# SwiGLU's first token group: block products of 256 columns in place of plain products of 512

## The chip, the cores and the metric

One Trainium2 chip (trn2), one of its cores. The metric is the device time of one execution in microseconds (us); lower is better.

## The reference

Three stages run one after the other on 2304 tokens (4 batches of 576) of width 512, in float32:

```python
q_s = softmax(q, axis=-1);  k_s = softmax(k, axis=2)          # with 1e-9 in the sums
x = einsum('bhsd,bhde->bhse', q_s, einsum('bhsd,bhse->bhde', k_s, v))   # 8 heads of 64
...
P = exp(x @ w_gate - max)                                     # 8 rounds of row and column scaling
for e in range(8):
    out += P[:, e:e+1] * (np.maximum(x @ w1[e], 0) @ w2[e])   # 512 -> 1024 -> 512
...
xn = x / np.sqrt(np.mean(x * x, -1) + 1e-6) * rms_g
g = xn @ w_gate;  val = xn @ w_val                            # 512 -> 1536
return (g / (1 + exp(-g)) * val) @ w_out                      # 1536 -> 512 (SwiGLU)
```

## The kernel before, in words

**Numbers in two halves.** Every large product is made of three matmuls: an operand is split into a high half (a copy rounded to fp32r) and a low half (what is left), and `mm3` (line 97) adds high x high, high x low and low x high in PSUM. So lines 98, 99 and 100 are nearly all of TensorE's work.

**Groups and units.** The 2304 tokens are cut into three groups of 512, 896 and 896 (`GP` holds half of each: 256, 448, 448). The hidden dimension is cut into chunks of 256: 32 units for each group in the mixture of experts (units 0 to 95), 6 for each group in SwiGLU (units 96 to 101 for the first group, 102 to 107, 108 to 113). A unit has two parts: `h`, its first products with what makes the hidden activations, and `y`, the second product that is added to the output rows. Parts stand in the program as h(u+1), y(u), h(u+2), y(u+1): the y of a unit lies behind the h of the next. Units 64 to 107 are one such stretch.

**Plain products and seven for eight.** The first token group takes its first products plainly: `plain` (line 824) multiplies chunk halves of 128 hidden columns with 512 tokens at a time, 24 matmuls for each weight matrix of a unit. The other groups use `seven` (line 772): the weights and the tokens are cut into 2 x 2 blocks, sums of blocks are formed beforehand, and seven block products (each 6 matmuls, here of 448 columns) stand for eight. What is left is put together from PSUM banks: `keep` copies a product on ScalarE, three additions run on VectorE (lines 795, 799, 804), one on GpSimd (line 805). Four banks are used: b1 twice, b2 and b3 once each. A product that adds to a bank waits until the copy from it is done, and one that takes a bank anew waits until the addition from it is done.

**SwiGLU units.** `unit2_h` (line 1019) does the gate matrix ("a"), then the value matrix ("v"). `gate_part` takes a sigmoid on ScalarE (line 1025) and multiplies on VectorE (line 1026); `value_part` multiplies (line 1029), rounds (line 1031) and takes the low half (line 1032). `unit2_y` adds into the output tiles (line 1077): 4 tiles of 128 tokens in the first group, 7 in the others.

**What is loaded when.** Block sums of tokens lie in seven tiles, `SX` (B11, T1, B21, T2, B22, T4, T3, in the order in which `seven` takes them). There is one buffer of each, so the sums of the next group can be loaded only when the last product of the group before has read its tile. In SwiGLU's second and third group they are read from DRAM by `sx_load` (line 718), 896 KB each. The block weights are read by `ws_load` (line 281), 896 KB for each half of a matrix, into two buffers; each load stands behind the product that frees its buffer. All these loads stand on one queue, SP, in the order of the program: an issue that has to wait holds up those behind it. The tokens of SwiGLU's first group come as plain halves from DRAM (`first_again`, line 975, into a slot kept as `X0`), written by `norm_first` (line 957) after the RMS norm of that group. Small steps (norms, block sums, second weights) are attached to places of units by `task` and `spread` (lines 1096 and 1222), called as `hook(i)`.

Of the kernel before, what the change touches and what calls it, by code (L numbers as in the profile page):

```python
# [18 lines left out]
def kernel(  # L19
# [260 lines left out]
    def ws_load(key):  # L280

        ws_alloc(key)
        for w, t in zip("hl", WS[key]):
            t = t.rearrange("p a k f -> p (a k f)").bitcast(F32)
            if key[1] < NU:
                nc.sync.dma_start(t, WSD[key + (w,)])
            else:
                g, c = divmod(key[1] - NU, NC2)
                d = WSD[key[0], c, w]
                if g:  # L290
                    nc.sync.dma_start(t, d[:, 2 * P:])
                else:
                    nc.sync.dma_start(t[:, :8 * P], d[:, :8 * P])
# [421 lines left out]
    def sx_alloc(nm, g):  # L715
        SX[nm] = sxp.tile([P, 2, 2, G], F32R, tag=nm, name=f"s{nm}_{g}")

    def sx_load(g, i):
        nm = NAMES[i]
        sx_alloc(nm, g)  # L720
        nc.sync.dma_start(SX[nm].rearrange("p w j n -> p (w j n)").bitcast(F32), SXD[nm, g])

    def sx_steps(g, j, b11, b21, b12, b22, stored):

        shp = b11.shape[1:]

# [3 lines left out]
        def put(nm, s):  # L730
            if stored:
                if j == 0:
                    SXD[nm, g] = dram.tile(
                        [P, 4 * G], F32, tag=f"{nm}{g}", name=f"sd{nm}_{g}"
# [3 lines left out]
                    f"{nm}_{g}_{j}", s, lambda t: v(t[:, :G]), lambda w: v(d[:, w, j]),  # L738
                    None if g == NG + 2 else staged,
# [32 lines left out]
    def seven(key, c, hook, after):  # L772

        wh, wl = WS.pop(key)
        nm = f"{key[0]}_{key[1]}"
        bk = {}
        tmp = {}

        def keep(n, i):
            tmp[n] = cp_.tile([P, G], F32, tag="u1" if n == "u3" else n, name=f"{n}_{nm}")  # L780
# [43 lines left out]
    def plain(u, f, key, stored):  # L824

        ph = bank("h", 2 * GP[0], f"ph_{key[0]}_{u}_{f}")
        plain_mm(ph, f, key, stored, range(KD))
        return ph

    def plain_mm(ph, f, key, stored, kks):  # L830
        wh, wl = WS[key]
        xh, xl = X0
        for kk in kks:
            if stored:
                i = ((2, 3), (0, 1))[f][kk // 2]
                lh, ll = wh[:, i, kk % 2], wl[:, i, kk % 2]
            else:
                lh, ll = (plain_view(t)[:, kk, f * P:(f + 1) * P] for t in (wh, wl))
# [10 lines left out]
    def unit_h(u, hook):  # L849
        if u < NCH:  # L850
            hook(0)
            for f in range(2):
                if f:
                    hook(1)
                if u == 0:
                    ph = FIRST_PH[f]
                    plain_mm(ph, f, ("a", 0), False, (KD - 1,))
                else:
                    ph = plain(u, f, ("a", u), False)
# [95 lines left out]
    XN0D = {}  # L955

    def norm_first(kk):

        pn = bank("y", DM, f"pn_0_{kk}")
        for t in range(TPG[0]):  # L960
            nc.tensor.transpose(
                pn[:, t * P:(t + 1) * P], ACC[0, 0][:, t, kk * P:(kk + 1) * P], ident
            )
        hi, lo = piece(f"xn0_{kk}")
        nc.scalar.activation(hi, pn, AF.Copy, scale=rmsg[:, kk:kk + 1])
        nc.vector.scalar_tensor_tensor(
            lo, pn, rmsg[:, kk:kk + 1], hi.bitcast(F32), op0=ALU.mult, op1=ALU.subtract
        )
        if kk == 0:
            XN0D[0] = dram.tile([P, 2 * KD * DM], F32, tag="xn0", name="xn0")  # L970
        d = XN0D[0].rearrange("p (w k n) -> p w k n", w=2, k=KD)
        for w, t in enumerate((hi, lo)):
            nc.sync.dma_start(d[:, w, kk], t.bitcast(F32))

    def first_again():
        nonlocal X0
        t = slot_a()
        nc.sync.dma_start(t.bitcast(F32), XN0D[0])
        X0 = as_x0(t)

# [4 lines left out]
    def norm_transpose(g, kk):  # L985
# [3 lines left out]
        for i in range(2):  # L989
# [14 lines left out]
        out_(0, 0, n, pns[0][:, :n * per])  # L1004
        out_(1, 0, 8 - n, pns[0][:, n * per:])
        out_(1, 8 - n, n, pns[1][:, :(2 * n - 8) * per])

    def norm_steps(g):
# [3 lines left out]
        if g == 0:  # L1012
            return steps + [lambda kk=kk: norm_first(kk) for kk in range(KD)]

# [4 lines left out]
    def unit2_h(u, hook):  # L1019
# [16 lines left out]
        cg = cp_.tile([P, 2, 2, G], F32, tag="c", name=f"cg_{u}")  # L1036
# [427 lines left out]
```

## Time and profile before

| | |
|---|---|
| device time, median of 3 runs | 2036.11 us (2035.25 to 2037.14) |
| the profiled execution, from its first to its last instruction (span) | 2033.2 us |
| median of the runs less that span | 2.9 us |
| TensorE matmuls | 2007.5 us busy, 99% of the span, 9522 instructions |
| VectorE, ScalarE, GpSimd | 69%, 38%, 20% of the span |
| DMA | 415 MB, mean 204 GB/s |

The profile gives the profiled execution by its span; it has no other time of its own. What lies around the span (2.9 us to the median) is taken as the same for both kernels. A matmul's record is longer than the distance to the next one, since matmuls overlap in the array; the distances of their starts tell what a stream of them costs.

### The profile page before, as it was taken

The numbers are of one execution on the slowest core, as the hardware profiler recorded it, in microseconds if no ns is written. First come the engines' busy times: TensorE is split into PE (matmuls) and PEld (weight loads), VectorE is DVE, ScalarE is ACT, GpSimd is POOL, SyncE is SP. The second block draws the span as 40 slices with busy tenths as digits, with TensorE's granted clock in tenths as the row PEclk, the third lists the DMA queues.
The fourth block names the chain that finished last, engine by engine and source line by source line (L and its number), as shares of the span: only waits on it lengthen the run. The fifth ranks groups of instructions, "written<-read, shape, count | busy, mean of one in ns | idle before, by whom it ended". The sixth has DMA issues, their size and how long they took to land.

```text
span 2033.2 us, 25609 instructions
## 1 busy us (share of the span) xinstructions
PE 2007.5 (99%) x9522; PEld 1739.5 (86%) x9522; DVE 1410.8 (69%) x2174; ACT 780.2 (38%) x1378; POOL 412.7 (20%) x388
## 2 busy tenths in 40 slices
PE   7999999999999999999999999999999999999999
PEld 5888888888888888888888888888888888888887
DVE  8775787776777777776658878878765446565455
ACT  5554333345333443343343333333332243432432
POOL 5541000022222222222113223223220000110110
PEclk9999999999999999999999999999999999999999
DMA  7443232355665665565677778878874747656542
GB/s 207 128 128 104 83 104 93 96 184 187 228 221 210 220 212 197 203 219 192 258 280 260 260 257 289 282 271 294 278 251 170 269 152 257 224 202 264 196 160 76
DMA packets 154236, 415.09 MB, mean 204 GB/s; under 512 B 13568, under 2 KB 66304, under 8 KB 153728
## 3 DMA queue, kind: packets, MB, share of 16 engines
q1 hardware_dynamic: 154112, 413.47, 58.7%
q8 instruction: 74, 1.21, 0.2%
q14 instruction: 50, 0.41, 0.1%
HBM read 281.69 MB, written 131.73 MB: 203 GB/s over the span
## 4 chain that ended last, share of the span: by engine, by line
PE 95%; DVE 4%; ACT 1%; issue 0%; DMA 0%; POOL 0%; DVEq 0%; POOLq 0%; ACTq 0%
PE py L98 13%; PE py L99 13%; PE py L100 13%; PE b_a L100 10%; PE b_a L99 10%; PE b_a L98 10%; PE ph_a L98 3%; PE ph_a L100 3%; PE ph_a L99 3%; PE po L98 2%; PE po L100 2%; PE po L99 2%; PE b_v L98 2%; PE b_v L100 2%; PE b_v L99 2%; PE pv L566 1%
## 5 line engine op out<-in xcount | busy, mean ns | idle before, releaser
L98 PE MATMUL py<-w2h,hh 128*128 128x512 f32 x1152 | 453.3, 393 | 3.4 <-DVE slot_e L905 1.9
L99 PE MATMUL py<-w2l,hh 128*128 128x512 f32 x1152 | 449.5, 390 | 0.0
L100 PE MATMUL py<-w2h,hl 128*128 128x512 f32 x1152 | 449.0, 390 | 0.0
L781 ACT COPY u_a<-b_a 128x448 f32<-128x448 f32 x228 | 121.6, 533 | 693.4 <-PE b_a L100 693.2
L98 PEld LDWEIGHTS py<-w2h,hh 128*128 128x128 f32 x1152 | 216.5, 188 | 47.5 <-DVE slot_e L905 2.1
L100 PEld LDWEIGHTS py<-w2h,hl 128*128 128x128 f32 x1152 | 216.6, 188 | 45.8
L99 PEld LDWEIGHTS py<-w2l,hh 128*128 128x128 f32 x1152 | 216.6, 188 | 42.9
L98 PE MATMUL b_a<-sT,wsh_a 128*128 128x448 f32 x608 | 220.0, 362 | 3.2 <-DVE c L795 2.1
L100 PE MATMUL b_a<-sT,wsl_a 128*128 128x448 f32 x608 | 220.7, 363 | 0.0
L99 PE MATMUL b_a<-sT,wsh_a 128*128 128x448 f32 x608 | 220.3, 362 | 0.0
L909 DVE SCALAR_TENSOR_TENSOR slot_a<-py,Pm,slot_a 128x512 f32<-128x512 f32 x217 | 162.4, 749 | 52.3 <-PE py L100 50.1
L909 DVE SCALAR_TENSOR_TENSOR slot_b<-py,Pm,slot_b 128x512 f32<-128x512 f32 x217 | 161.1, 745 | 23.6 <-PE py L100 22.5
L100 PE MATMUL b_a<-sB,wsl_a 128*128 128x448 f32 x456 | 165.7, 363 | 0.3 <-DMA wsl_a<-wdl_a 0.3
L99 PE MATMUL b_a<-sB,wsh_a 128*128 128x448 f32 x456 | 165.2, 362 | 0.0
L98 PE MATMUL b_a<-sB,wsh_a 128*128 128x448 f32 x456 | 165.2, 362 | 0.0
L95 DVE TENSOR_TENSOR w2l<-w2r,w2h 128x512 fp32r<-128x512 f32 x162 | 118.0, 729 | 41.4 <-ACT w2h L94 41.4
L805 POOL TENSOR_TENSOR c<-u_a,p_a 128x448 f32<-128x448 f32 x64 | 73.9, 1155 | 344.2 <-ACT u_a L781 344.1
L843 DVE SCALAR_TENSOR_TENSOR hl<-c,hh 128x896 fp32r<-128x896 f32 x128 | 143.0, 1117 | 0.9 <-ACT hh L842 0.7
L240 POOL TENSOR_TENSOR sum<-w1r 128x256 f32<-128x256 f32 x32 | 23.7, 741 | 565.2 <-DMA w1r<-in_moe_w_dram 247.1
L842 ACT ACTIVATE hh<-c 128x896 fp32r<-128x896 f32 x128 | 122.4, 956 | 27.9 <-POOL c L805 27.9
L94 ACT CAST w2h<-w2r 128x512 fp32r<-128x512 f32 x162 | 97.1, 618 | 88.9 <-PE py L100 80.7
L98 PEld LDWEIGHTS b_a<-sT,wsh_a 128*128 128x128 f32 x608 | 113.7, 187 | 13.1 <-DVE c L795 3.7
(232 smaller groups left out, 3675.4 us busy)
## 6 DMA issues: line engine op xcount, KB each, us to landing
w2r<-in_moe_w_dram SPq DMA_DIRECT2D x96, 512.0 KB, 4.6
w1r<-in_moe_w_dram SPq DMA_DIRECT2D x64, 512.0 KB, 3.5
wsdh<-wsh_a SPq DMA_DIRECT2D x32, 896.0 KB, 6.5
wsdl<-wsl_a SPq DMA_DIRECT2D x32, 896.0 KB, 7.9
wsh_a<-wsdh SPq DMA_DIRECT2D x32, 896.0 KB, 6.7
wsl_a<-wsdl SPq DMA_DIRECT2D x32, 896.0 KB, 8.4
w2d<-w2l SPq DMA_DIRECT2D x32, 512.0 KB, 2.9
w2l<-w2d SPq DMA_DIRECT2D x32, 512.0 KB, 4.8
```

The costliest lines, as they stand in the source:

```text
L94: nc.scalar.copy(hi, src)
L95: (eng or nc.vector).tensor_tensor(lo, src, hi.bitcast(F32), op=ALU.subtract)
L98: nc.tensor.matmul(ps, lh, rh, start=first, stop=False, skip_group_check=True)
L99: nc.tensor.matmul(ps, lh, rl, start=False, stop=False, skip_group_check=True)
L100: nc.tensor.matmul(ps, ll, rh, start=False, stop=last, skip_group_check=True)
L240: nc.gpsimd.tensor_tensor(s1, a21, a22, op=ALU.add)
L566: nc.tensor.matmul(st["pv"][:, :P], st["ke"][:, c].rearrange("p h d -> p (h d)"), st["v"][:, :, c, :], start=(c == 0), stop=(c == SC - 1),)
L781: nc.scalar.copy(tmp[n], bk[i])
L805: nc.gpsimd.tensor_tensor(c[:, 1, 1], tmp["u3"], tmp["p5"], op=ALU.add)
L842: nc.scalar.activation(th, src, AF.Relu)
L843: return lambda: nc.vector.scalar_tensor_tensor(tl, src, 0.0, th.bitcast(F32), op0=ALU.max, op1=ALU.subtract)
L909: nc.vector.scalar_tensor_tensor(a, py, pe, a, op0=ALU.mult, op1=ALU.add)
```

## The change

The first token group's SwiGLU units take `seven` as well, with block columns of 256 tokens: 42 matmuls of 256 columns for each matrix instead of 24 of 512. Its normed tokens are formed into block sums and stored in DRAM, seven pairs of halves, instead of the plain halves; `norm_first` and `first_again` go away. The weights' load is the same for all groups now (14 blocks instead of 8 for the first). The block sums of the first group are loaded in unit 95, tile by tile as its products free them (512 KB each), and those of the second group in the value products of unit 101 (hooks 7 to 13); before, those of the second group were all loaded at the start of unit 96. The sums of the first group take 51 small steps, which now lie in units 32 to 38 (before 16 steps in units 34 to 37), and the next group's first steps begin two units later.

```diff
@@ ws_load
-                g, c = divmod(key[1] - NU, NC2)
+                c = (key[1] - NU) % NC2
                 d = WSD[key[0], c, w]
-                if g:
-                    nc.sync.dma_start(t, d[:, 2 * P:])
-                else:
-                    nc.sync.dma_start(t[:, :8 * P], d[:, :8 * P])
+                nc.sync.dma_start(t, d[:, 2 * P:])
...
@@ sx_alloc, seven
+        w = GP[g % NG]
+        t = sxp.tile([P, 4 * G], F32R, tag=nm, name=f"s{nm}_{g}")[:, :4 * w]
...
-                bk[b] = pb_tile(f"b{b}", f"b{b}_{nm}_{i}")[:, :G]
+                bk[b] = pb_tile(f"b{b}", f"b{b}_{nm}_{i}")[:, :w_]
...
@@ norm_transpose, norm_steps
-        for i in range(2):
+        for i in range(1 if g == 0 else 2):
...
+        if g == 0:
+            out_(1, 0, n, pns[0][:, n * per:])
+            return
...
-        if g == 0:
-            return steps + [lambda kk=kk: norm_first(kk) for kk in range(KD)]
-
         steps += [lambda kk=kk: norm_transpose(g, kk) for kk in range(KD)]
         return steps + sx_all(g + NG, lambda kk, h: norm_place(g, kk, h), True)
...
@@ unit2_h
-        if g == 0:
-            for f in range(2):
-                hook(f)
-                to = cg[:, f].rearrange("p t g -> p (t g)")[:, :n]
-                gate_part(plain(u, f, ("a", u), True), to, f)
...
-            return
...
+        cg = four(cp_.tile([P, 2, 2, G], F32, tag="c", name=f"cg_{u}"))
+        cv = four(cp2.tile([P, 2, 2, G], F32, tag="cv", name=f"cv_{u}"))
         hook(-1)
         seven(("a", u), cg, hook, lambda f: gate_part(flat(cg, f), flat(cg, f), f))
...
@@ tasks
-            task("h", u, (0 if group(u)[0] == 0 else 4) + f, lambda u=u, f=f: w2_split(u, f))
+            task("h", u, 4 + f, lambda u=u, f=f: w2_split(u, f))
...
-    spread([("h", u, i) for u in range(34, 38) for i in (0, 1, 3, 4)], lambda: norm_steps(0))
+    spread(
+        [at for u in range(33, 39) for at in
+         [("h", u, i) for i in (0, 1, 3, 4)] + [("y", u - 1, i) for i in range(6)]][6:],
+        lambda: norm_steps(0),
+    )
...
-        [("y", u, i) for u in range(39, 57) for i in (3, 5)],
+        [("y", u, i) for u in range(41, 59) for i in (3, 5)],
...
-    task("y", NU - 3, 0, first_again)
     for i in range(7):
-        task("h", NU, 0, lambda i=i: sx_load(NG + 1, i))
+        task("h", NU - 1, i, lambda i=i: sx_load(NG, i))
+    for i in range(7):
+        task("h", NU + NC2 - 1, 7 + i, lambda i=i: sx_load(NG + 1, i))
```

TensorE, at the start of unit 96's gate products. Before (`ph` is the bank, `slot_a` the tokens, `wsh` and `wsl` the two halves of the weights):

```order
L98 MATMUL ph_a_96_0_14271<-slot_a_14060,wsh_a_96_14047 128x512
L99 MATMUL ph_a_96_0_14271<-slot_a_14060,wsh_a_96_14047 128x512
L100 MATMUL ph_a_96_0_14271<-slot_a_14060,wsl_a_96_14048 128x512
...
L98 MATMUL ph_a_96_1_14291<-slot_a_14060,wsh_a_96_14047 128x512
L99 MATMUL ph_a_96_1_14291<-slot_a_14060,wsh_a_96_14047 128x512
```

Now, the last two products of the gate and the first of the value matrix of the same unit (half of each product's six matmuls; b1 and b2 are banks, sT4, sT3 and sB11 the block sums of the tokens):

```order
L98 MATMUL b2_a_96_5_14393<-sT4_3_14257,wsh_a_96_14129 128x256
L99 MATMUL b2_a_96_5_14393<-sT4_3_14257,wsh_a_96_14129 128x256
L100 MATMUL b2_a_96_5_14393<-sT4_3_14257,wsl_a_96_14130 128x256
...
L98 MATMUL b1_a_96_0_14348<-sT3_3_14279,wsh_a_96_14129 128x256
L99 MATMUL b1_a_96_0_14348<-sT3_3_14279,wsh_a_96_14129 128x256
L100 MATMUL b1_a_96_0_14348<-sT3_3_14279,wsl_a_96_14130 128x256
...
L98 MATMUL b1_v_96_0_14424<-sB11_3_14201,wsh_v_96_14275 128x256
L99 MATMUL b1_v_96_0_14424<-sB11_3_14201,wsh_v_96_14275 128x256
L100 MATMUL b1_v_96_0_14424<-sB11_3_14201,wsl_v_96_14276 128x256
```

Each matmul has 256 columns instead of 512, and its own load of weights; the T3 product adds to the bank of product 0, and the value products follow at once.

SP, the queue of loads, around unit 101, the last of the first group. Before (w2r is the raw second weight, sd and s the block sums in DRAM and in SBUF; unit 102's sums are not among these rows, since they were loaded in unit 96):

```order
L293 DMA wsh_v_101_14943<-wdh_v_5_13248 128x1024
L293 DMA wsl_v_101_14944<-wdl_v_5_13249 128x1024
L387 DMA sdB21_5_14502<-pch_B21_5_0_14922 128x448
L387 DMA sdB21_5_14502<-pcl_B21_5_0_14923 128x448
L179 DMA w2r_102_15005<-w32_0_9884 128x1024
L291 DMA wsh_a_102_15024<-wdh_a_0_9422 128x1792
L291 DMA wsl_a_102_15025<-wdl_a_0_9423 128x1792
```

Now:

```order
L179 DMA w2r_102_15454<-w32_0_9966 128x1024
L290 DMA wsh_a_102_15469<-wdh_a_0_9504 128x1792
L290 DMA wsl_a_102_15470<-wdl_a_0_9505 128x1792
L720 DMA sB11_4_15482<-sdB11_4_9294 128x1792
L720 DMA sT1_4_15493<-sdT1_4_9297 128x1792
L720 DMA sB21_4_15503<-sdB21_4_9295 128x1792
L720 DMA sT2_4_15513<-sdT2_4_9299 128x1792
L720 DMA sB22_4_15522<-sdB22_4_9296 128x1792
L720 DMA sT4_4_15536<-sdT4_4_9300 128x1792
L290 DMA wsh_v_102_15552<-wdh_v_0_9774 128x1792
L290 DMA wsl_v_102_15553<-wdl_v_0_9775 128x1792
L720 DMA sT3_4_15556<-sdT3_4_9298 128x1792
```

Seven loads of block sums have moved in here, six between unit 102's gate weights and its value weights, and T3's behind both.

VectorE, in unit 97. Before (cg and cv hold gate and value, hl the low half of the activations, w2l that of the second weights):

```order
L95 TENSOR_TENSOR w2l_97_14409<-w2r_97_14289,w2h_97_14408 128x512
L1026 TENSOR_TENSOR cg_97_14407<-ph_a_97_0_14412,sg_97_0_14425 128x512
L95 TENSOR_TENSOR w2l_97_14409<-w2r_97_14289,w2h_97_14408 128x512
L1026 TENSOR_TENSOR cg_97_14407<-ph_a_97_1_14432,sg_97_1_14445 128x512
L1029 TENSOR_TENSOR cg_97_14407<-ph_v_97_0_14452,cg_97_14407 128x512
```

Now (u1, u2 and u3 are ScalarE's copies, b2 and b3 banks):

```order
L798 TENSOR_TENSOR cg_97_14552<-b2_a_97_2_14572,u1_a_97_14561 128x256
L802 TENSOR_TENSOR cg_97_14552<-b3_a_97_1_14563,u2_a_97_14586 128x256
L95 TENSOR_TENSOR w2l_97_14596<-w2r_97_14405,w2h_97_14595 128x512
L999 TENSOR_TENSOR cg_97_14552<-cg_97_14552,sg_97_0_14606 128x512
L95 TENSOR_TENSOR w2l_97_14596<-w2r_97_14405,w2h_97_14595 128x512
L807 TENSOR_TENSOR cg_97_14552<-b2_a_97_5_14599,u3_a_97_14619 128x256
L999 TENSOR_TENSOR cg_97_14552<-cg_97_14552,sg_97_1_14623 128x512
L798 TENSOR_TENSOR cv_97_14553<-b2_v_97_2_14648,u1_v_97_14637 128x256
```

The addition that frees bank b2 for the value products now stands behind one multiplication and both splits of the second weights.

## Rows read from the trace of the kernel before

**Rows 1.** The page: busy time of each engine, and the chain that ended last.

```profile
PE 2007.5 (99%) x9522; PEld 1739.5 (86%) x9522; DVE 1410.8 (69%) x2174; ACT 780.2 (38%) x1378; POOL 412.7 (20%) x388
...
PE 95%; DVE 4%; ACT 1%; issue 0%; DMA 0%; POOL 0%; DVEq 0%; POOLq 0%; ACTq 0%
```

**Rows 2.** Waits of TensorE from 1560 us on: who waited for what, total us, times, longest.

```profile
PE b_a L98 <- ACT u_a L781: 1.0, 1, 1.0
PE b_a L100 <- DMA wsl_a<-wdl_a: 0.3, 1, 0.3
```

**Rows 3.** Timeline of TensorE, SwiGLU's first group, around unit 97: start us, duration.

```profile
1617.66 0.39 PE L98 MATMUL ph_a<-slot_a,wsh_a 128*128 128x512 f32 x1
...
1628.54 0.39 PE L98 MATMUL po<-w2h,hh 128*128 128x512 f32 x1
...
1633.98 0.39 PE L98 MATMUL ph_a<-slot_a,wsh_a 128*128 128x512 f32 x1
```

**Rows 4.** The same timeline in the second group: matmuls of 448 columns.

```profile
1737.72 0.36 PE L98 MATMUL b_v<-sT,wsh_v 128*128 128x448 f32 x1
...
1741.92 0.39 PE L98 MATMUL po<-w2h,hh 128*128 128x512 f32 x1
```

**Rows 5.** The same timeline in the attention: twelve short matmuls and what follows.

```profile
106.06 1.50 PE L566 MATMUL pv<-v,ke 96*128 96x128 f32 x12
107.39 0.28 PE L578 MATMUL pv<-ones,s 96*128 96x1 f32 x2
```

**Rows 6.** The same timeline in unit 107: first value product, first output product.

```profile
1839.65 0.36 PE L98 MATMUL b_v<-sB,wsh_v 128*128 128x448 f32 x1
...
1848.24 0.39 PE L98 MATMUL po<-w2h,hh 128*128 128x512 f32 x1
```

**Rows 7.** Timeline of SP there: issue us, duration of the issue.

```profile
1840.88 0.32 SPq L179 DMA_DIRECT2D w2r<-w  x1
1841.31 0.37 SPq L291 DMA_DIRECT2D wsh_a<-wdh_a  x1
...
1842.21 0.42 SPq L721 DMA_DIRECT2D sB<-sdB  x1
...
1847.24 0.32 SPq L721 DMA_DIRECT2D sT<-sdT  x1
...
1851.47 0.32 SPq L721 DMA_DIRECT2D sT<-sdT  x1
```

**Rows 8.** DMA issues of 1842.21, 1847.24 and 1851.47: KB, us to landing.

```profile
sB<-sdB SPq DMA_DIRECT2D x1, 896.0 KB, 9.2
...
sT<-sdT SPq DMA_DIRECT2D x1, 896.0 KB, 15.3
...
sT<-sdT SPq DMA_DIRECT2D x1, 896.0 KB, 18.5
```

**Rows 9.** Groups by line and shape: busy us, mean ns, idle before.

```profile
L643 ACT CAST slot_a<-px 128x256 fp32r<-128x256 f32 x8 | 2.7, 374 | 0.8 <-PE px L628 0.7
...
L1025 ACT ACTIVATE sg<-ph_a 128x512 f32<-128x512 f32 x12 | 7.2, 598 | 15.8 <-PE ph_a L100 15.8
...
L650 DVE TENSOR_TENSOR slot_a<-px,slot_a 128x256 fp32r<-128x256 f32 x8 | 2.9, 408 | 0.7 <-ACT slot_b L645 0.7
...
L95 DVE TENSOR_TENSOR w2l<-w2r,w2h 128x512 fp32r<-128x512 f32 x162 | 118.0, 729 | 41.4 <-ACT w2h L94 41.4
...
L1026 DVE TENSOR_TENSOR cg<-ph_a,sg 128x512 f32<-128x512 f32 x12 | 8.3, 692 | 16.9 <-ACT sg L1025 16.9
...
L240 POOL TENSOR_TENSOR sum<-w1r 128x256 f32<-128x256 f32 x32 | 23.7, 741 | 565.2 <-DMA w1r<-in_moe_w_dram 247.1 <-issue 194.3 <-ACT p_a L781 108.2
```

**Rows 10.** Windows: busy us by engine, granted clock, DMA share, GB/s.

```profile
500.00:620.00 120.00, 118.89 (x562) 103.95 (x563) 86.06 (x120) 48.05 (x78) 30.63 (x31) 1.00 0.65 232
...
142.00:146.00 4.00, 3.43 (x9) 2.73 (x10) 3.53 (x7) 1.78 (x5) 1.52 (x3) 0.57 0.68 204
```

**Rows 11.** Timeline of TensorE at that clock: a matmul behind a gap.

```profile
142.57 0.79 PE L98 MATMUL py<-w2h,hh 128*128 128x512 f32 x1 [1.18 <-DVE late L905]
```

More of the change, by code (lines that the diff above doesn't have):

```diff
@@ L733, in put @@
                     SXD[nm, g] = dram.tile(
-                        [P, 4 * G], F32, tag=f"{nm}{g}", name=f"sd{nm}_{g}"
+                        [P, 4 * n], F32, tag=f"{nm}{g}", name=f"sd{nm}_{g}"
                     )
@@ L737, in put @@
                 return list(halves(
[L738 to L739 removed]
+                    f"{nm}_{g}_{j}", s, lambda t: v(t[:, :n]), lambda w: v(d[:, w, j]),
+                    None if g in (NG, NG + 2) else staged,
                 ))
@@ L775, in seven @@
         nm = f"{key[0]}_{key[1]}"
+        w_ = GP[group(key[1])[0]]
         bk = {}
@@ L779, in keep @@
         def keep(n, i):
-            tmp[n] = cp_.tile([P, G], F32, tag="u1" if n == "u3" else n, name=f"{n}_{nm}")
+            tmp[n] = cp_.tile(
+                [P, G], F32, tag="u1" if n == "u3" else n, name=f"{n}_{nm}"
+            )[:, :w_]
             nc.scalar.copy(tmp[n], bk[i])
@@ L822, in h_tiles, with plain, plain_mm @@
         return t
-    def plain(u, f, key, stored):
+    def plain(u, f, key):
         ph = bank("h", 2 * GP[0], f"ph_{key[0]}_{u}_{f}")
-        plain_mm(ph, f, key, stored, range(KD))
+        plain_mm(ph, f, key, range(KD))
         return ph
-    def plain_mm(ph, f, key, stored, kks):
+    def plain_mm(ph, f, key, kks):
         wh, wl = WS[key]
@@ L833, in plain_mm @@
         for kk in kks:
[L834 to L838, printed above, removed]
+            lh, ll = (plain_view(t)[:, kk, f * P:(f + 1) * P] for t in (wh, wl))
             mm3(ph, lh, ll, xh[:, kk], xl[:, kk], kk == 0, kk == KD - 1)
@@ L856, in unit_h @@
                     ph = FIRST_PH[f]
-                    plain_mm(ph, f, ("a", 0), False, (KD - 1,))
+                    plain_mm(ph, f, ("a", 0), (KD - 1,))
                 else:
-                    ph = plain(u, f, ("a", u), False)
+                    ph = plain(u, f, ("a", u))
                 relu(*h_tiles(u, f), ph)()
@@ L953, in norm_scale @@
         nc.vector.tensor_scalar_mul(a, a, SS[g][:, t:t + 1])
[L955 to L979, printed above, removed]
     def norm_place(g, kk, h):
@@ L1034, in value_part @@
             )
-        cg = cp_.tile([P, 2, 2, G], F32, tag="c", name=f"cg_{u}")
-        if g == 0:
-            for f in range(2):
-                hook(f)
-                to = cg[:, f].rearrange("p t g -> p (t g)")[:, :n]
-                gate_part(plain(u, f, ("a", u), True), to, f)
-            del WS["a", u]
-            hook(2)
-            for f in range(2):
-                hook(3 + f)
-                to = cg[:, f].rearrange("p t g -> p (t g)")[:, :n]
-                value_part(plain(u, f, ("v", u), True), to, f)()
-            del WS["v", u]
-            hook(5)
-            return
+        w = GP[g]
+        four = lambda t: t.rearrange("p f t g -> p (f t g)")[:, :4 * w].rearrange(
+            "p (f t g) -> p f t g", f=2, t=2
+        )
         flat = lambda t, f: t[:, f].rearrange("p t g -> p (t g)")
-        cv = cp2.tile([P, 2, 2, G], F32, tag="cv", name=f"cv_{u}")
+        cg = four(cp_.tile([P, 2, 2, G], F32, tag="c", name=f"cg_{u}"))
+        cv = four(cp2.tile([P, 2, 2, G], F32, tag="cv", name=f"cv_{u}"))
         hook(-1)
@@ L1162 @@
         i = 6 if kd == "a" else 13
-        if u >= NU and group(u)[0] == 0:
-            i = 2 if kd == "a" else 5
         task("h", u, i, lambda key=key: ws_load(key))
```

10 lines of the change are left out of this document (6 added, 4 removed).

## The prediction, on record before the changed kernel ran

> **What bounds the kernel now.** I read the page first: TensorE is busy for 99% of the span, and 95% of the chain that ended last is its own work [rows 1]. Then its waits from 1560 us on, the stretch that the change touches: 1.3 us in all [rows 2]. So time there is won or lost on TensorE alone: by fewer columns, or by a wait that was not there. Then the timelines, for what a stream of matmuls costs. In the first group's units 48 matmuls of 512 columns take 10.88 us (1617.66 to 1628.54) and the 24 of a y part 5.44 us [rows 3]: 0.2267 us each. In the second group 21 matmuls of 448 columns take 4.20 us [rows 4]: 0.200 us each. Last SP's timeline and the landings at the change from the second to the third group, where the kernel before already does what the change adds between first and second [rows 7, 8].
>
> **Products (faster).** From 448 to 512 columns a matmul grows by 26.7 ns, 0.417 ns a column; 192 columns below 448 that gives 0.200 - 0.080 = 0.120 us for 256, an estimate on the straight line through the two rows. 42 of them take 5.04 us where 24 of 512 take 5.44: 0.40 us saved for each of 12 matrices, 4.8 us in all. The saving is small because seven for eight gives 12.5%, and a cost of 13 ns that hangs on each matmul, not on its columns, eats half of it. No row shows 256 columns of this type. The nearest short stream is the attention's: 12 in 1.33 us, 0.111 each, weights loaded for each [rows 5]. That is the lower end (4.66 us a matrix, 9.4 us saved). The upper end is the record of a weight load, 1739.5 / 9522 = 0.183 us [rows 1], if loads could not overlap one another; the attention's stand closer [rows 5], so I take 0.120. The last of the 12, unit 101's value matrix, lies in the stretch that I cost by the loads, so 11 x 0.40 = **-4.4 us** here.
>
> **Waits on the narrow products (slower).** A product now lasts 0.72 us (6 x 0.120) instead of 1.2, while what ScalarE and VectorE do between products shrinks less. Follow a unit from the end of gate product 4 (0); results are there 0.16 us after the next matmul starts (0.36 long, 0.20 apart [rows 4]). VectorE, at 0.41 for 256 columns, 0.69 and 0.73 for the multiplication and a split of 512 [rows 9]: the addition 0.16 to 0.57, a split to 1.30, the gate's multiplication to 1.99, the second split to 2.72, the addition that frees b2 to 3.13. TensorE wants b2 for value product 2 at 1.44 + 1.44 = 2.88: 0.25 us of waiting. ScalarE's second sigmoid must wait for that addition and GpSimd's (0.74 us), runs to 3.73, and the copy of value product 0 stands behind it (0.37, to 4.10), while product 3 wants to add to that bank at 3.85: 0.25 more. So 0.5 us a unit, in units 96 to 100 **+2.5 us** (unit 101's is covered by the loads). Units 99 and 100 carry the third group's norm steps besides, five a unit of 0.4 to 0.7 us each (an estimate from the widths in [rows 9]) on VectorE or ScalarE between the same products; I take **+1 us** for both. Ends: 0, if the order loosens, and 6 us.
>
> **The loads at the second group's start (slower, the largest term).** Seven loads of 896 KB stood at the start of unit 96, with six units ahead of their use. Now each waits for a value product of unit 101, and only y(100) with its 24 matmuls lies between that and unit 102, which reads them. In their midst on SP stand the weights of unit 102 (four loads of 896 KB), and T3, the last sum, stands behind the value weights. Exactly this train runs before at unit 107, only there two y parts of 7 tiles follow (19 us), and nothing waited. Its times: gate products end, and value products begin, at 1839.65 [rows 6]; the split of w2 holds SP until 1840.88, the gate weights go out at 1841.31, 1.66 us after that end [rows 7]. B11 (issued 1842.21) lands 9.2 us later at 1851.4, T4 (1847.24) at 1862.5, five loads further: 2.2 us each. T3 (1851.47) lands at 1870.0 [rows 7, 8]. Counted from the end of the gate products: B11 at 11.8, then one each 2.2 us to T4 at 22.9, the two value weights, T3 at 30.4.
> In the changed unit 101 VectorE works through the same steps ahead of w2r (2.72 - 1.44 = 1.3 us after the gate's end, and the issue), so I take the same 30.4; subtractions for the third group in that unit could add 1 to 2. TensorE is at unit 102 after 5.04 + 0.5 + 5.44 = 11.0 us, waits some 0.8 for B11, then about 1.0 ahead of each product (1.2 us of work, a load each 2.2), ends product 5 at 24.1 and waits 6.3 for T3. Unit 102's gate is done at 30.4 + 1.2 = 31.6 us; before, the same stretch takes 5.44 + 5.44 + 42 x 0.2 = 19.3. **+12.3 us**. Nothing later can give it back, as TensorE is the bound on both sides. Lower end: T3 not held up by the two value weights, 4.5 us less; upper: 2 more.
>
> **The clock.** A short gap shows what follows such a wait: 1.18 us idle behind a run of very short matmuls [rows 11], and over 142 to 146 us the granted clock is 0.57 on average, 1.2 instead of 2.4 GHz for most of it [rows 10]: 4 x 0.43 = 1.7 us lost. The wait for T3 is five times as long, so I take **+1.7 us** once; ends 0 (it falls in the wait itself) and 3.4 (twice).
>
> **What costs nothing.** Within the first group a unit moves four weight loads (3.67 MB) and w2r in some 16 us; the train above moves 0.92 MB per 2.2 us, so they land in about 10 us. The first group's own sums (3.67 MB) have two product lengths and a y part of 7 tiles to come in, over 16 us, with 6 MB in all: also covered. Without cover, each late load costs 2.2. The norm of the first group adds 14 low halves and 10 subtractions of 256 columns and takes away four of 512: some 7 us on VectorE in units 32 to 38, where it has 28% free (86 of 120 us busy [rows 10]). I take 0, with 2 as the upper end; the late one would be the addition that frees a bank. The reload of the plain halves (2 MB) was hidden, so its going gains nothing.
>
> **Sum.** -4.4 + 2.5 + 1.0 + 12.3 + 1.7 = +13.1 us. The span would be 2046.3 instead of 2033.2; with the 2.9 us around it, from the median of 2036.1 to **2049 us**.
>
> A rule of the Trainium skill speaks for a still longer train. The train shows 0.92 MB in 2.2 us, 417 GB/s [rows 7, 8]. The page DMA: Bandwidth & Descriptors (Specifications) puts the HBM limit of a core at about 358 GB/s; by it a load would take 2.56 us (estimate from that page), the eleven behind the first 4 us more, and the sum would be +17. The trace disagrees with the rule, so it has a small chance below.
>
> **Rivals.**
> - The loads come in time. For: nothing waits for these loads anywhere before [rows 2]. Against: this needs T3 some 12 us earlier than it came before [rows 7, 8]; the wait vanishes only if it lands within 11.0 + 7.2 = 18.2 us of the gate's end. Without the narrow products' waits the time is 2036.1 - 4.8 = 2031.3, **faster**; with them (3.5) 2034.8, no change. 5% and 4%.
> - T3 overtakes the value weights, since its issue stands right behind theirs: 25.9 instead of 30.4, 2044.7. Against: landings in the train keep the order of issue. 6%.
> - Weight loads bound the narrow matmuls at 0.183 us: 7.69 us a matrix, 11 x 2.25 = 25 us more than before, with the train and the clock 2075. Against: the short stream [rows 5]. 3%.
> - The slower train, loads of 2.56 us: 2053. By the page's rule above. 2%.
>
> **How the numbers follow.** The forecast gets 80%. Its range: lower end +12.3 with 0.111 us a matmul (11 x 0.78 = 8.6 saved), no other waits, 2039.8, which I cut to 2040.5 since all ends at once are unlikely; upper end -4.4 + 6 + 14.3 + 3.4 + 2 = +21.3, 2057. It takes in the overtaking and the slower train; the weight-load case and the faster ones stay out. A measurement of this kernel can tell 0.2%, 4 us, from no change: faster 5%, within it 4%, slower 91%.
>
> **What would show it.** TensorE's waits name DMA of sT and sB in unit 102, 10 to 12 us in all, the longest about 6, on the product of T3; before that product the clock falls once. The 256-column matmuls start 0.12 us apart; their waits name u1, c's additions or the sigmoid's chain, about half a microsecond a unit. A first group whose waits are larger than the saving, or a unit 102 without a wait for DMA, would prove me wrong: the first on the chains, the second on the whole sign.

## The result, and the profile after

The changed kernel takes 2050.53 us in the median of 4 runs (2050.07 to 2053.8); the kernel before, on the same chip, 2036.62. **It is slower by 13.9 us**, where 13.1 was predicted, and the time lies in the range. The ratio is 1.0071 [1.0059, 1.0083], an interval of 12 to 17 us.

The page of the changed kernel: busy time, and the chain that ended last.

```profile
PE 2011.9 (98%) x9738; PEld 1748.7 (85%) x9738; DVE 1428.9 (70%) x2228; ACT 800.1 (39%) x1444; POOL 425.1 (21%) x400
...
PE 90%; DVE 3%; DMA 3%; ACT 2%; issue 1%; POOL 0%; SPq 0%; DVEq 0%; POOLq 0%; ACTq 0%
```

Against [rows 1] TensorE is busy for 4.4 us more, not less (in part because matmuls at a lower clock last longer, as the timeline below shows), and its share of the chain fell from 95% to 90%, while DMA rose from 0 to 3% and ScalarE from 1 to 2%. TensorE's waits from 1560 us on say which (us in total, times, longest):

```profile
PE b_a L98 <- DMA sT<-sdT: 6.6, 3, 5.1
PE b_v L98 <- DVE cg L807: 3.4, 4, 1.1
PE b_a L98 <- DMA sB<-sdB: 2.1, 3, 0.8
PE b_a L98 <- ACT u_a L784: 1.5, 2, 1.2
PE b_v L98 <- ACT u_v L784: 1.0, 5, 0.2
PE b_a L98 <- DVE cg L802: 0.7, 1, 0.7
PE pn L965 <- DVE slot_b L952: 0.6, 1, 0.6
```

In [rows 2] the same stretch had two waits, 1.3 us. The two kinds that were forecast are both here: sB and sT are the second group's sums (8.7 us), cg and u the chains between narrow products. TensorE's timeline, first in unit 96:

```profile
1598.73 0.28 PE L98 MATMUL b_a<-sB,wsh_a 128*128 128x256 f32 x1
...
1603.68 0.28 PE L98 MATMUL b_v<-sB,wsh_v 128*128 128x256 f32 x1
...
1606.31 0.39 PE L98 MATMUL b_v<-sB,wsh_v 128*128 128x256 f32 x1 [1.06 <-DVE cg L807]
1606.54 0.28 PE L99 MATMUL b_v<-sB,wsh_v 128*128 128x256 f32 x1
...
1607.48 0.38 PE L98 MATMUL b_v<-sT,wsh_v 128*128 128x256 f32 x1 [0.20 <-ACT u_v L784]
...
1610.41 0.39 PE L98 MATMUL py<-w2h,hh 128*128 128x512 f32 x1
```

The gate matrix runs through in 4.95 us, 0.118 a matmul. The value matrix takes 6.73, though its two waits record only 1.26 us of idle time: the rest, 0.52, lies at the two restarts. The idle record begins only where the last matmul's record ends (0.28 long), while in a stream the next one starts 0.118 after it, so each wait costs 0.16 more than its record; and the first matmul behind a wait is slow (0.39 instead of 0.28, and the next starts 0.23 later), 0.11 more. The first wait stands behind VectorE's multiplication, which waits for a sigmoid behind a table load on ScalarE; the second behind the second sigmoid, which waits for GpSimd's addition (their timelines):

```profile
1602.67 1.28 ACT L998 ACT_TABLE_LOAD   x1
```

```profile
1605.45 1.05 POOL L808 TENSOR_TENSOR cg<-u_a,p_a 128x256 f32<-128x256 f32 x1 [14.30 <-ACT u_a L784]
```

Then unit 102:

```profile
1708.26 0.44 PE L98 MATMUL b_a<-sB,wsh_a 128*128 128x448 f32 x1 [0.63 <-DMA sB<-sdB]
...
1710.41 0.44 PE L98 MATMUL b_a<-sT,wsh_a 128*128 128x448 f32 x1 [0.70 <-DMA sT<-sdT]
...
1719.19 0.44 PE L98 MATMUL b_a<-sT,wsh_a 128*128 128x448 f32 x1 [0.73 <-DVE cg L802]
...
1725.74 0.71 PE L98 MATMUL b_a<-sT,wsh_a 128*128 128x448 f32 x1 [5.11 <-DMA sT<-sdT]
...
1728.12 0.57 PE L98 MATMUL b_v<-sB,wsh_v 128*128 128x448 f32 x1
```

A product starts every 2.2 us although it needs 1.2, and the seventh stands until T3 is there. (The wait of 1719.19 is put down to VectorE, but T4's load, issued at 1701.89, landed 17.2 us later, at 1719.09, right ahead of it; it is a wait for a load, like its neighbours.) SP's timeline shows the train (issue us, duration):

```profile
1699.38 0.32 SPq L720 DMA_DIRECT2D sB<-sdB  x1
...
1703.76 0.32 SPq L290 DMA_DIRECT2D wsh_v<-wdh_v  x1
1705.92 0.32 SPq L290 DMA_DIRECT2D wsl_v<-wdl_v  x1
1708.14 0.32 SPq L720 DMA_DIRECT2D sT<-sdT  x1
```

The issue of 1708.14 is T3. It took 17.5 us to land, at 1725.64, right ahead of the product that starts at 1725.74 (DMA issues: KB, us to landing):

```profile
sT<-sdT SPq DMA_DIRECT2D x1, 896.0 KB, 17.5
```

The windows of that stretch (busy us by engine, granted clock, DMA share, GB/s):

```profile
1708.00:1724.00 16.00, 8.70 (x36) 6.29 (x36) 5.05 (x8) 4.51 (x8) 0.00 (x0) 1.00 1.02 422
1724.00:1731.00 7.00, 5.26 (x14) 4.72 (x15) 0.62 (x1) 1.27 (x2) 1.15 (x1) 0.53 0.79 278
```

The DMA engines are full, at 422 GB/s, while TensorE is busy for 8.70 of 16 us, not at all in the last three; then the clock stands at 1.2 GHz for nearly 7 us, the last part of the wait and the work behind it.

The lengths of TensorE's parts, read from the starts in its timeline, put all kernels of this study side by side (us). "To 102" goes from unit 96's first gate product to unit 102's first, "gate" and "value" are unit 102's, and the total is their sum, up to unit 102's y part.

| kernel | to 102 | gate | value | total | ratio to before |
|---|---|---|---|---|---|
| before | 105.18 | 8.41 | 8.60 | 122.19 | 1 |
| after | 109.53 | 19.86 | 9.89 | 139.28 | 1.0071 |
| e1 loads late, plain products | 105.19 | 20.34 | 10.10 | 135.63 | 1.0072 |
| e2 after, sums ahead | 108.97 | 8.40 | 9.33 | 126.70 | 1.0019 |
| e3 after, splits early | 109.50 | 19.89 | 8.98 | 138.37 | 1.0075 |
| e4 both | 108.62 | 8.41 | 8.58 | 125.61 | 1.0011 |
| e5 after, T3 first | 109.47 | 15.25 | 14.39 | 139.11 | 1.0075 |
| e6 e2, splits and sigmoid moved | 103.27 | 8.41 | 10.03 | 121.71 | 0.9995 |
| e7 e6, splits earlier | 105.49 | 8.41 | 9.86 | 123.76 | 1.0005 |
| e8 e6, second weight last | 103.25 | 8.41 | 8.44 | 120.10 | 0.9982, 0.9988 |
| e9 e8, norm steps earlier | 106.08 | 8.41 | 8.45 | 122.94 | 0.9994 |
| e10 e8, squares earlier | 101.95 | 8.41 | 8.55 | 118.91 | 0.9978 |

The totals follow the ratios within some 3 us. One difference has no part in the change: in the profiled execution of after the clock fell once more in the attention, at 86 to 93 us (0.76 over that window, 1.00 before), and unit 96 starts 1.5 us later. The clock fell there in the profiled executions of e1 (0.80) and e2 (0.76) too, and not in e3 (1.00). That execution is the longest of the four; its span is 18.7 us above [rows 1]'s, where the medians differ by 13.9.

### The profile page after: what moved, and what is told of

Same layout as the page of the kernel before. It is cut to its first block, busy times and chain, and to the rows that moved or that the text cites. A ratio compares the mean times of both kernels' runs of the same rounds, so it can differ in the third digit from the quotient of the medians.

```text
span 2051.9 us, 26287 instructions
## 1 busy us (share of the span) xinstructions
PE 2011.9 (98%) x9738; PEld 1748.7 (85%) x9738; DVE 1428.9 (70%) x2228; ACT 800.1 (39%) x1444; POOL 425.1 (21%) x400
## 4 chain that ended last, share of the span: by engine, by line
PE 90%; DVE 3%; DMA 3%; ACT 2%; issue 1%; POOL 0%; SPq 0%; DVEq 0%; POOLq 0%; ACTq 0%
PE py L98 12%; PE py L99 12%; PE py L100 12%; PE b_a L100 10%; PE b_a L98 10%; PE b_a L99 10%; PE ph_a L98 3%; PE ph_a L100 3%; PE ph_a L99 3%; PE po L98 2%; PE po L99 2%; PE po L100 2%; PE b_v L98 2%; PE b_v L100 2%; PE b_v L99 2%
## 5 line engine op out<-in xcount | busy, mean ns | idle before, releaser
L784 ACT COPY u_a<-b_a 128x448 f32<-128x448 f32 (+1 forms) x246 | 128.3, 522 | 708.9 <-PE b_a L100 705.9
L98 PE MATMUL b_a<-sT,wsh_a 128*128 128x448 f32 (+1 forms) x656 | 234.5, 357 | 10.5 <-DMA sT<-sdT 6.6
L100 PE MATMUL b_a<-sT,wsl_a 128*128 128x448 f32 (+1 forms) x656 | 234.5, 357 | 0.0
L99 PE MATMUL b_a<-sT,wsh_a 128*128 128x448 f32 (+1 forms) x656 | 234.1, 357 | 0.0
L98 PE MATMUL b_a<-sB,wsh_a 128*128 128x448 f32 (+1 forms) x492 | 175.5, 357 | 2.1 <-DMA sB<-sdB 2.1
L908 DVE SCALAR_TENSOR_TENSOR slot_b<-py,Pm,slot_b 128x512 f32<-128x512 f32 x217 | 161.1, 745 | 22.9 <-PE py L100 22.0
L100 PE MATMUL b_a<-sB,wsl_a 128*128 128x448 f32 (+1 forms) x492 | 175.7, 357 | 0.1
L99 PE MATMUL b_a<-sB,wsh_a 128*128 128x448 f32 (+1 forms) x492 | 175.3, 356 | 0.0
L98 PEld LDWEIGHTS b_a<-sT,wsh_a 128*128 128x128 f32 x656 | 123.0, 187 | 22.4 <-issue 8.7
L99 PEld LDWEIGHTS b_a<-sT,wsh_a 128*128 128x128 f32 x656 | 123.4, 188 | 8.6
```

The source lines that it names most:

```text
L98: nc.tensor.matmul(ps, lh, rh, start=first, stop=False, skip_group_check=True)
L99: nc.tensor.matmul(ps, lh, rl, start=False, stop=False, skip_group_check=True)
L100: nc.tensor.matmul(ps, ll, rh, start=False, stop=last, skip_group_check=True)
L908: nc.vector.scalar_tensor_tensor(a, py, pe, a, op0=ALU.mult, op1=ALU.add)
```

## The experiments

**e1_plain_late_sums: the late loads alone.** The kernel before, with only the second group's sums moved into unit 101.

```diff
-        task("h", NU, 0, lambda i=i: sx_load(NG + 1, i))
+        task("h", NU + NC2 - 1, 5 if i == 6 else 2, lambda i=i: sx_load(NG + 1, i))
```

> The kernel before, with its plain products of 512 columns, and only the seven loads of the second group's block sums moved from the start of unit 96 into unit 101, in the order that the changed kernel has them (six behind the gate weights of unit 102, T3 behind its value weights). No narrow product is in it. My theory, that the train of loads is the largest term: TensorE waits in unit 102 for sums, mostly for T3, and the time rises by 9 to 13 us over the kernel before, to 2045.5 to 2049.5 (a little less than in the changed kernel, since the split of the second weights no longer holds the queue there). The rival, that the products of 256 columns and their larger weight loads cost most: under 4 us over the kernel before, 2040 or less.

Measured: 2050.66 us against 2036.46, 1.0072 [1.0058, 1.0085]. That is the loss of the whole change, from the loads alone, a little above the range of the theory. Its waits:

```profile
PE b_a L98 <- DMA sT<-sdT: 6.8, 3, 5.1
PE b_a L98 <- DMA sB<-sdB: 1.4, 2, 0.7
PE b_a L98 <- ACT u_a L781: 1.2, 1, 1.2
```

The clock took more than in after: 0.61 over 14 us.

```profile
1712.00:1726.00 14.00, 7.40 (x21) 5.92 (x22) 3.06 (x5) 3.39 (x6) 0.04 (x1) 0.61 0.91 358
```

What follows: the late loads alone cost as much as the whole change, within the intervals (each some 5 us wide). That the narrow products bring nothing net is not shown by it: in the table after's total is 3.7 us longer than e1's, and e2 measures what they cost without the train.

**e2_sums_ahead: the loads taken out of the train.** After, with four of the first group's sums in the slot that used to hold its plain halves, so that four buffers of the second group can be filled from unit 96 on; of the three left, T3 goes ahead of the value weights.

```diff
+        if g == NG and i < 4:
+            if i == 0:
+                FIRST4.append(slot_a())
+            t = FIRST4[0][:, i * 4 * w:(i + 1) * 4 * w]
...
-        task("h", NU + NC2 - 1, 7 + i, lambda i=i: sx_load(NG + 1, i))
+        if i < 4:
+            task("h", NU, 0, lambda i=i: sx_load(NG + 1, i))
+        elif i < 6:
+            task("h", NU + NC2 - 1, 7 + i, lambda i=i: sx_load(NG + 1, i))
+    TASK["h", NU + NC2 - 1, 13].insert(0, lambda: sx_load(NG + 1, 6))
...
```

> The changed kernel with its products, but four of the first group's seven sums (B11, T1, B21, T2; 16 KB a partition) lie in the slot that held the plain halves before, so the second group's four are loaded in unit 96; of the other three, T3's load goes ahead of the value weights. Only three loads of sums are left in the train, in time by the landings of the changed kernel (B22 12.6, T4 14.8 and T3 17 us after the gate's end at the latest, wanted at 16.7, 17.9 and 19.1). My theory: the waits for sums and the fall of the clock go, 13.3 + 1.3 us by the trace, less about 1 for the value weights: 2036.5 to 2041, with the waits inside the narrow products left. The rival, that narrow products cost most: 2046 or more.

Measured: 2040.39 us, 1.0019 [1.0010, 1.0029], in the theory's range. Gate 102 is back at 8.40 us and the clock does not fall behind it. The waits that are left are mostly the narrow products' own; value 102 (9.33) still waits for the second half of its weights:

```profile
PE b_v L98 <- DVE cg L816: 3.2, 4, 1.0
PE b_v L98 <- ACT u_v L793: 1.0, 5, 0.2
...
PE b_v L100 <- DMA wsl_v<-wdl_v: 0.6, 1, 0.6
```

So nearly three quarters of the loss are the train; the rest, by "to 102" 3.8 us and 0.7 in value 102, is in the main that the narrow products wait for more than they save.

**e5_t3_first: only the order of the train.** After, with T3's load ahead of unit 102's value weights.

```diff
-        task("h", NU + NC2 - 1, 7 + i, lambda i=i: sx_load(NG + 1, i))
+        if i < 6:
+            task("h", NU + NC2 - 1, 7 + i, lambda i=i: sx_load(NG + 1, i))
+    TASK["h", NU + NC2 - 1, 13].insert(0, lambda: sx_load(NG + 1, 6))
```

> The changed kernel with one thing altered: the load of T3 stands ahead of unit 102's two value weights instead of behind them. The train keeps its length; only its last three loads change places. My theory, that the end of the train sets the end of the wait: T3 lands about 4.4 us earlier, but the low half of the value weights now lands last, where T3 did (30 us after the gate's end), and the third matmul of the value product needs it, so the gate's end comes 4 us earlier and the value product waits instead. Gain: one product (1.2 us) that now lies ahead of the last landing, and as the longest wait shrinks from 5.1 to about 2 us, perhaps the fall of the clock (up to 2.7 us by the trace): 2046.5 to 2049. The rival, that T3's own lateness is the cost: 4.4 us and the clock, 2043.5 to 2046.

Measured: 2051.45 us, 1.0075 [1.0061, 1.0088]. Both missed: nothing is gained. Gate 102 falls from 19.86 to 15.25 us, and the value part rises from 9.89 to 14.39, since the value weights are now what is last:

```profile
PE b_v L100 <- DMA wsl_v<-wdl_v: 3.0, 1, 3.0
PE b_a L98 <- DMA sT<-sdT: 2.2, 3, 0.8
```

The two parts together are 29.64 instead of 29.75 us. The train's length sets its end, whatever stands last in it. The clock fell all the same, behind a wait of 3.0 us instead of 5.1: it was granted at 0.50 from 1726 to 1732 us.

**e3_split_early: the order on VectorE.** After, with the two splits of the second weights at the gate's first two hooks, so that the addition that frees b2 no longer stands behind them.

```diff
-            task("h", u, 4 + f, lambda u=u, f=f: w2_split(u, f))
+            task("h", u, (0 if group(u)[0] == 0 else 4) + f, lambda u=u, f=f: w2_split(u, f))
```

> The changed kernel, with the two splits of the second weights of the first group's units moved from hooks 4 and 5 to hooks 0 and 1 of the gate products. My theory: VectorE reaches the addition that frees b2 about 1.4 us earlier, so the waits for it (3.4 us by the trace, with restarts about 5) go, and the train of loads starts about 1.3 us earlier, since the queue no longer waits for the second split: 3 to 6 us less than the changed kernel, 2044.5 to 2047.5. The rival, that these waits only move on to ScalarE's and GpSimd's part of the chain: less than 2 us, 2048.5 or more.

Measured: 2051.45 us, 1.0075 [1.0062, 1.0089]. The theory missed, and the time lies in the rival's range, though the waits moved to another place than it named. Most value matrices fall to 5.4 us, but the gates of units 96 to 99 rise from 4.95, 4.95, 5.54 and 5.11 to 5.28, 5.28, 6.51 and 6.24, because the same splits now stand ahead of the gate's own addition:

```profile
PE b_a L98 <- DMA sT<-sdT: 6.6, 3, 5.1
PE b_a L98 <- DVE cg L798: 2.7, 4, 1.0
```

"To 102" stays at 109.50. Moving work from one narrow product to the next moves the wait with it.

**e4_ahead_and_early: e2 and e3 together.**

> Both edits together on the changed kernel: four sums ahead, T3 ahead of the value weights, the splits early. If the loads and the waits on b2 are all that the change cost, what is left is the saving of 42 x 0.118 against 24 x 0.227 us for each of 12 matrices (5.9 us) less some waits on ScalarE (1 to 3 us): 2033 to 2036.5, at or below the kernel before. The rival, that something else in the narrow products costs (restarts, weight loads): 2038 or more.

Measured: 2038.18 us, 1.0011 [1.0002, 1.0020]. The theory missed; the number is the rival's, but for the reason that e3 shows and not for one that no order could change (e6): the gates are 5.23 to 6.49 us in units 96 to 99. Gates 98 and 99 show a second cause. The third group's squares (0.64 us each, with 0.20 to read the sum out) stand on ScalarE among the evictions of the y part, and ScalarE has them done only at 1634.4 us, when gate 98, begun at 1632.2, already waits for its first copy.

**e6_where_there_is_room and e7_sigmoid_later.** Both have e2's loads, and put the sigmoid of the gate's second half behind the value matrix's first two copies and its multiplication behind the first addition. e6 puts one split in the gate and one in the value matrix; e7 both at the gate's very start.

```diff
...
+        def value_hook(i):
+            to = flat(cg, 1)
+            if g == 0 and i == 1:
+                sg.append(gate_sigmoid(to, 1))
+            elif g == 0 and i == 2:
+                nc.vector.tensor_tensor(to, to, sg[0], op=ALU.mult)
+            hook(7 + i)
...
-            task("h", u, 4 + f, lambda u=u, f=f: w2_split(u, f))
+            task("h", u, (2 + 7 * f if group(u)[0] == 0 else 4 + f), lambda u=u, f=f: w2_split(u, f))
```

> The second experiment (four sums ahead, T3 ahead of the value weights), with the order of the narrow products' helpers altered in the first group: the splits of the second weights lie behind the additions of gate product 2 and value product 2, where VectorE has a gap; the sigmoid of the gate's second half stands behind ScalarE's first two copies of the value products instead of ahead of them, its multiplication behind the value's first addition. My theory, that order alone makes the waits: the gate and value products of units 96, 97 and 101 come to about 4.95 us each (42 x 0.118) instead of 4.95 and 6.2; units 98 to 100 keep some waits from the third group's norm on ScalarE. 12 x 0.49 saved less 2 to 3 us: 2032 to 2035, faster than the kernel before. The rival, that narrow products bring restarts that no order removes: 2037 or more.

> As the one with the helpers where there is room, except that both splits of the second weights stand at the head of each first-group unit, ahead of gate product 0 and behind it. If ScalarE is late from the third group's norm in the y parts ahead of units 98 to 101, the splits' copies at the head delay the first copies and additions of the gate, and its products wait as in the fourth experiment: 2034 to 2037, 1 to 3 us above the one with room. The rival, that only the sigmoid's place matters: the same as that one within 1 us.

Measured: e6 2034.93 us against 2035.62, 0.9995 [0.9986, 1.0003]; e7 2035.85, 1.0005 [0.9996, 1.0015]; both in their ranges. That e6 is faster than the kernel before, as its text has it, is not shown: its interval takes in 1. And the two times do not tell e7's theory from its rival, since they lie 0.9 us apart; the totals in the table, 2.0 apart, speak for the theory. In e6 six of the twelve matrices run through at 5.0 us, the others take 5.2 to 6.7, and TensorE's waits for ScalarE's copies and VectorE's additions sum to 1.3 us:

```profile
PE b_v L100 <- DMA wsl_v<-wdl_v: 1.4, 1, 1.4
PE b_a L100 <- DMA wsl_a<-wdl_a: 0.9, 1, 0.9
PE b_a L98 <- ACT u_a L793: 0.8, 2, 0.4
PE pn L974 <- DVE slot_b L961: 0.7, 1, 0.7
PE b_v L98 <- DVE cg L816: 0.5, 2, 0.3
```

In e7 the splits stand ahead of ScalarE's copies and VectorE's additions at the gates instead (gates up to 6.22 us in units 96 to 99). The longest wait of e6 is again a train: the value weights' second half, behind a second weight and three sums.

**e8_short_train: the last wait of the train.** As e6, with unit 102's second weight loaded behind its value weights, and with its two splits moved from the gate to the value products of that unit.

```diff
-            if u + 1 < ALL:
+            if u + 1 < ALL and u + 1 != NU + NC2:
...
-            task("h", u, (2 + 7 * f if group(u)[0] == 0 else 4 + f), lambda u=u, f=f: w2_split(u, f))
+            task("h", u, (2 + 7 * f if group(u)[0] == 0 else 4 + f + (7 if u == NU + NC2 else 0)), lambda u=u, f=f: w2_split(u, f))
...
+    task("h", NU + NC2, 0, lambda: w2_load(NU + NC2))
```

> The kernel of e6_where_there_is_room, with the load of unit 102's second weight put behind its value weights instead of ahead of them, so that one load of 6.8 MB less moved per engine stands before the value weights' second half. Theory (the order of the train sets the one wait that is left there): the wait of 1.4 us on the value weights' second half goes, the value part of unit 102 falls from 10.0 to about 8.6 us, and the time is 0.7 to 1.5 us below e6's: 2033.4 to 2034.9, with the kernel before near 2035.6. Rival (the train is as long as before, and the wait moves to the y part's second weight or to the next unit's sums): within 0.7 us of e6's.

(The load that moves is of 512 KB; the 6.8 MB of that text is a slip.) Measured: 2033.27 us against 2037.2, 0.9982 [0.9973, 0.9991]. That is a little below the theory's range, beside a kernel before that was slower than e6's. Value 102 falls from 10.03 to 8.44 us, and no wait for value weights is left. As a ratio it is 2.6 us below e6, more than the 1.6 that the trace shows. A second measurement, beside e10:

> The kernel of e8_short_train once more, beside the next one on the same chip. Theory (its saving is 2 us in the first group and nothing elsewhere): 0.998 to 0.9995 of the kernel before's time, and the first group's stretch 103.3 us again. Rival (the earlier run's 0.9982 was in part luck): 0.9995 or more.

Measured: 2034.17 us against 2036.02, 0.9988 [0.9979, 0.9997], "to 102" 103.25. In both measurements it is faster than before, by 3.7 and 2.4 us; the trace's totals give 2.1.

**e9_squares_ahead and e10_squares_alone: ScalarE's backlog.** Both begin the third group's norm in unit 95. In e9 every step moves forward; in e10 only the first twelve places do. The edit of e10, as against e8:

```diff
-        [("y", NU + i // 4, i % 4) for i in range(12)]
+        [("y", NU - 1, i) for i in range(1, 7)] + [("y", NU + i // 4, i % 4) for i in range(6)]
```

> As e8_short_train, and the squares of the third group's norm begin a unit earlier, in the y part of unit 95, so that ScalarE has none of them in units 98 to 100. Theory (the rest of the waits on the narrow products, gates of 5.3 to 6.7 and values of 5.4 to 5.6 us where 5.0 are needed, is ScalarE's lateness behind those squares): units 98 to 101 give back about 1 us, the first group's stretch to unit 102's gate falls from 103.3 to 102.3 us or less, and the time is 0.7 to 2 us below e8's: 2031.5 to 2034, faster than before. Rival (the squares only move their cost to units 95 to 97, or VectorE and not ScalarE is what is late): within 0.7 us of e8's.

> As e8_short_train, and only the squares of the third group's norm begin a unit earlier (six steps in unit 95, the next six in units 96 and 97); its transposes, their evictions and the splits behind them stay in the places of e8_short_train, where e9_squares_ahead had moved them a unit forward too. Theory (ScalarE's squares at the end of units 97 and 98 are what make gates 98 and 99 longer than 5.0 us): gate 98 falls from 5.68 to about 5.0 us and gate 99 from 5.29 to about 5.0, the first group's stretch to unit 102's gate from 103.25 to 102.2 to 102.6 us, and the time is 0.5 to 1.5 us below e8's, 0.9968 to 0.9982 of the kernel before's. Rival (what e9_squares_ahead lost came with the squares, not with the transposes and splits): the stretch is 104 us or longer, and the time is above e8's.

Measured: e9 2036.09 us, 0.9994 [0.9985, 1.0003], and "to 102" 106.08, worse than e8, which took 2033.27 beside it: the theory missed, and its rival too. Its transposes fell into gate 99 (8.66 us), and the casts of its block sums into gate 100 and value 100 (7.47 and 6.94), where ScalarE was late: a cast held it for 3.25 us, since its buffer was still being stored (ScalarE's timeline).

```profile
PE b_a L98 <- ACT u_a L793: 2.6, 2, 2.2
```

```profile
1673.78 0.56 ACT L377 CAST pch_B<-slot_b 128x448 fp32r<-128x448 f32 x1 [3.25 <-DMA sdB<-pch_B]
```

e10: 2031.36 us, 0.9978 [0.9968, 0.9988], and "to 102" 101.95, 1.3 us below e8 in the trace. The time is the theory's; the mechanism is so only in part, since its text is wrong on one point: the steps are one list, so the first transposes moved as well, from the y part that follows unit 99's products into gate 99, which rose to 6.92 while that y part fell from 7.96 to 5.48. Of the 1.3 us, 0.9 are from this pair, which the theory did not have in it. Gate 98 fell only to 5.36; a table load and two evictions stood ahead of the copy that it waits for, as ScalarE's timeline shows:

```profile
1631.37 1.28 ACT L949 ACT_TABLE_LOAD   x1
1632.66 0.21 ACT L949 ACTIVATE rt<-ms 128x7 f32<-128x7 f32 x1
1632.77 1.06 ACT L1062 COPY slot_e<-po 128x512 f32<-128x512 f32 x2
1633.72 0.39 ACT L793 COPY u_a<-b_a 128x256 f32<-128x256 f32 x1
```

What remains on TensorE from 1560 us on in e10:

```profile
PE b_a L98 <- ACT u_a L793: 0.7, 1, 0.7
PE b_a L100 <- DMA wsl_a<-wdl_a: 0.5, 1, 0.5
PE pn L974 <- DVE slot_b L961: 0.2, 1, 0.2
PE b_v L98 <- DVE cg L816: 0.2, 1, 0.2
```

e10 is the fastest kernel of the study, 0.22% [0.12, 0.32] below the kernel before and 0.9% below after by the two ratios.

## Why the prediction was right

The sign, the place and the size of the largest term held, because it was read from a train that the kernel before already ran. The term of the waits on the narrow products did not, and by the prediction's own sign (waits in the first group larger than the saving) it was wrong on the chains. By its steps, in the profiled execution:

- **Products, -4.4.** 0.118 us a matmul where 0.120 was estimated, and 4.95 us a matrix: 0.49 saved instead of 0.40, 5.4 for eleven. The estimate on the straight line through 448 and 512 columns was good; the attention's 0.111 [rows 5], a row of 128 columns and not of 256, was no measure of it, and weight loads did not bound the stream, since a matmul starts every 0.118 us where a load's record was 0.183.
- **Waits on the narrow products, +2.5 and +1.** This is the term that was mis-sized. From unit 96's start to the end of gate 101 after takes 96.79 us (1598.73 to 1695.52), before 94.30 (1597.26 to 1691.56): with 5.4 saved, the waits cost **7.9**, not 3.5, and more than the 5.4 saved. Of them 6.2 lie in the value matrices and 1.4 in the gates of units 98 to 100. Values 97 and 98 are 0.8 above 4.95, as compared with the 0.5 forecast; part of it is the restart behind each wait. Values 96, 99 and 100 are 1.8, 1.6 and 1.2 above. The chain was right up to its first sigmoid, but in unit 96 a table load of 1.28 us (at 1602.67) stands ahead of it, which the forecast had left out, and GpSimd's addition took 1.05 us instead of 0.74. In unit 99 the norm's root, at 1652.71, is followed by such a load ahead of the sigmoid again. That the order of these steps is the cause is shown by e6, which gives back 5.7 us of "to 102" against e2 by moving splits and sigmoid alone, and by e3, where a different order moves the waits.
- **Loads, +12.3.** From the end of gate 101 T3 lands at 30.1 us, where 30.4 was taken from [rows 7, 8]; gate 102 ends at 32.6 instead of 19.3. 12.1 of these 13.3 us are the train and 1.2 the clock in the last product (2.38 us instead of 1.2). e1 shows the term by itself. The waits for sums are 9.4 us with T4's, below the 10 to 12 that were named, and the one for T3 was 5.1 instead of 6.3, because T4 landed 23.6 us after the gate's end instead of 22.9 and its product ended later; the end is the same, since the train sets it.
- **The clock, +1.7.** It fell once, in the wait for T3. 1.2 us in that product and 1.3 in value 102 (9.89 against 8.60): 2.5, inside the ends 0 to 3.4. In e1 it took more (1.5 us in value 102 alone), in e2, where the wait is gone, nothing.
- **What costs nothing.** The norm in units 32 to 38 and the first group's own sums: TensorE has no wait between 500 and 700 us, and unit 96 starts without one. The reload's going gained nothing that the trace shows.
- **The rivals.** "The loads come in time" is excluded by after and by e1; e2 and e6 show that its condition was the right one but its prices too low, by the same waits: with the loads in time and the waits as they are it is 1.0019 (e2, 3.9 us slower, where 1.3 us faster was given), and without most of the waits 0.9995 (e6, 1.0 us faster, where 4.8 was given). The overtaking is excluded by T3's landing at 1725.64, behind the second half of the value weights (issued at 1705.92, 17.5 us to landing), and e5 shows that even the better order would have gained nothing: the price of 4.5 us that the prediction put on it was wrong, as the value weights would have become the last. The slower train is excluded by 422 GB/s and by a product every 2.2 us.

The sum of the profiled execution is +1.5 (attention) + 2.5 + 13.3 + 1.3 = 18.6 of 18.7. Without the attention the terms sum to -5.4 + 7.9 + 12.1 + 2.5 = 17.1 where 13.1 was forecast, and nearly all of the 4.0 between is the mis-sized waits. That the forecast lies within 0.8 us of the medians' 13.9 is therefore luck in part; the traced total is that of the longest execution, and how the other three divide their time was not traced.

## What to carry to other kernels

Where tiles have one buffer each, look for the last reader of the old contents and the first of the new, and count every load between them on that queue, others' loads too: a train that ran unseen under 19 us of other work is bare under 11. A saving of 0.4 us a matrix is only had if every engine between two products has less to do than the product lasts; count table loads and the restart behind each wait, and expect that moving a step can move its wait to the next product (e3, e9) until a place with room is found (e6). Changing the order inside a train that is longer than the work it must hide under only renamed the last wait here (e5); taking loads out of it, or starting them a stage earlier, removes it.

## What the runs showed of the hardware

- A wait of TensorE costs more than its idle record: about 0.26 us more in unit 96 (6.73 - 4.95 - 1.26 = 0.52 for two), 0.16 for the overlap of two records in a stream (0.28 long, 0.118 apart) and 0.11 for a first matmul that the next one follows 0.23 us later.
- A stream of these matmuls costs 0.118 us at 256 columns, with weights loaded for each, beside 0.200 at 448 and 0.2267 at 512 [rows 3, 4]: the straight line through those two gives 0.120 for 256.
- A train of 896 KB loads runs at 422 GB/s for 16 us with the DMA engines full.
- After 16 us in which TensorE was busy for 8.70, the last three of them idle, the clock stood at 1.2 GHz for nearly 7 us (0.53 granted over 1724 to 1731), in part while TensorE still waited; in e1 it averaged 0.61 over 14 us, and in e2, without the wait, it stayed at 1.00.
